# Weight halves in a three-buffer staging pool, a fourth buffer in five pools, casts and copies dealt out anew to ScalarE and VectorE, q of two more tiles by DMA transpose

## The chip, the cores and the metric

The kernel runs on one core of one Trainium2 chip. The core has four compute engines that the profile names PE (matrix multiply), DVE (vector), ACT (activation) and POOL (GpSimd), and SP, which here only issues DMAs. Each engine takes its instructions in its own fixed order and waits on semaphores for the others. The metric is the device time of one execution in microseconds. The kernel before took 172.4 us (median of 4 runs, 172.18 to 172.47).

## The reference

Attention with a sliding window of 128 positions and 4 sink positions, and after it a channel mix. There are 4 sequences of 768 positions, 8 heads of 64, so a model width of 512; the inner width of the mix is 1024.

```python
scores = q @ k.T / sqrt(64)                 # per sequence and head
keep = is_sink | (0 <= row - col < 128)
a = exp(where(keep, scores, -1e9)); a = a / a.sum()
x = (a @ v)                                 # heads side by side: [4, 768, 512]
x_prev = x shifted down by one position (0 at the start)
xk = mu_k * x + (1 - mu_k) * x_prev
xr = mu_r * x + (1 - mu_r) * x_prev
out = sigmoid(xr @ w_r) * (relu(xk @ w_k) ** 2 @ w_v)
```

All inputs and the output are float32.

## The kernel before

The positions are cut into 12 units of 256 (three a sequence, `U = 12`, u counts them). For each unit the program does this, in bf16 with sums in fp32:

- **Load and prepare** (`load`, L354; `prepare`, L516). k, q and v of the unit come in as fp32 (tiles `ks`, `qs`, `vs`), all on SP's queue. k and q are cast to bf16 by halves of four heads (`kb`, `qb`, L526 and L529: one helper, two layouts), and turned so that the head dimension lies on partitions (`kt`, `qt`). That is done in one of two ways. Either PE does four 128x128 transposes a half into a PSUM bank (L550) and another engine copies the bank out (`evacuate`, L560); or, for the units in `KD` and `QD`, a transposing DMA on SP does it (L537, `DMA_TRANSPOSE` in the profile). For such units k or q is loaded in two DMAs of 256 KB, otherwise in one of 512 KB. v is cast in two halves (`vb`, L575).
- **Attend** (`attend`, L613). Scores for two head pairs at once (L635, into `sc`), exponential on ACT (`e`, L657), times a mask on DVE (L671), value products on PE (L694, and for the sinks L682), then on DVE the reciprocal of the row sum (`rec`, L707) and the multiply (`x`, L710). A unit that is not first in its sequence also reads k and v of the unit before, and the sinks' scores (L611, `es`).
- **Mix** (`mix`, L719). PE transposes x (L733), a copy brings it to `xt` (L744), DVE takes the difference with the previous position (`td`, L758) and makes `xk` and `xr` (L768, eight instructions a unit).
- **The products** (`ffn`, L807). Key products (L818, 32 matmuls a unit in four groups of two), ReLU on ACT (`rl`, L827), square on DVE (`kk`, L831), gate products (L841, tanh on ACT L847), output products (L859) and the last multiply (`ob`, L868), which SP stores (L875).

The weights come once. `wk32`, `wr32` and `wv32` hold them whole in fp32; they are loaded in five DMAs of 1 MB (L397) and cast in ten pieces on DVE (`cast`, L492).

The order of the work is not left to a scheduler at run time. The program first records every operation in a list (class `Plan`, `op`, L135), numbered as they are recorded, with its engine, cost, the tiles that it takes from a pool, and what it reads and writes. `ORDER` (L43) is a table of these numbers for each engine, written out by hand or by a search: each engine issues its operations in just that order. `schedule` (L141) walks the five lists with the costs to decide how the lists interleave, which buffer of a pool each operation gets, and where PE would be idle for more than 0.3 to 0.6 us; there it puts a fill, a matmul on a constant tile `warm` (L879) whose result is not used. Fills are put only in the first 45 us of its reckoning. Where a pool has no free buffer, an operation waits for the one that held it.

Engines are given by small tables: `CAST` and `CAST0` (casts of k and q; the second for unit 0), `EVAC0` (copies from PSUM of unit 0; ACT for all others), `WCAST` (weights: all DVE), `VCAST` (v: DVE for unit 0, POOL for the others). `KD` is units 4 to 11, `QD` units 8 to 11.

Of the kernel before, what the change touches and what calls it, by code (L numbers as in the profile page):

```python
# [17 lines left out]
CAST = {"k": "ACT", "q": "ACT"}  # L18

CAST0 = {"k": "DVE", "q": "DVE"}  # L20
EVAC0 = {"k": "ACT", "q": "DVE", "x": "ACT"}

KD = range(4, 12)
QD = range(8, 12)
# [11 lines left out]
LOADS = ("kq0", "v0", "kq1", "wka", "v1", "wkb", "wr", "wva", "wvb")  # L36
WCAST = ("DVE",) * 10
VCAST = ("DVE", "POOL")
# [6 lines left out]
        92, 89, 98, 105, 95, 116, 108, 113, 128, 141, 124, 119, 131, 137, 103, 148, 134, 157,  # L45
        155, 168, 219, 211, 207, 212, 220, 208, 160, 176, 165, 171, 183, 189, 215, 193, 200,
        223, 180, 216, 225, 237, 298, 186, 290, 302, 291, 303, 299, 294, 248, 295, 227, 235,
        231, 263, 232, 228, 260, 306, 266, 318, 240, 256, 245, 251, 310, 276, 269, 311, 283,
        326, 329, 308, 321, 314, 343, 315, 370, 378, 352, 366, 371, 379, 332, 367, 374, 382,
        337, 375, 384, 359, 348, 386, 396, 387, 421, 390, 274, 444, 391, 452, 445, 453, 426,  # L50
        407, 448, 456, 394, 449, 457, 460, 399, 464, 404, 465, 415, 462, 410, 430, 472, 499,
        578, 437, 468, 474, 504, 469, 525, 583, 526, 537, 485, 538, 533, 509, 529, 534, 530,
        477, 553, 482, 488, 493, 545, 511, 564, 518, 549, 541, 546, 543, 550, 601, 609, 605,
        602, 556, 610, 606, 567, 631, 613, 561, 572, 614, 617, 587, 619, 621, 594, 629, 622,
        634, 625, 639, 626, 642, 677, 689, 678, 681, 663, 690, 682, 645, 707, 685, 650, 686,
        695, 701, 670, 718, 705, 702, 693, 697, 710, 698, 760, 715, 761, 756, 768, 757, 769,
        721, 726, 764, 742, 765, 772, 749, 740, 784, 780, 774, 781, 795, 834, 830, 835, 842,
        831, 787, 843, 838, 792, 798, 860, 776, 803, 816, 839, 777, 823, 846, 848, 854, 858,
        855, 871, 910, 918, 906, 911, 907, 850, 863, 851, 919, 868, 936, 874, 914, 879, 915,
        930, 892, 924, 899, 931, 926, 947, 934, 922, 944, 939, 927, 976, 972, 977, 984, 973,  # L60
        985, 950, 980, 955, 958, 981, 988, 990, 965, 992, 996, 993, 997, 1012, 1000, 1013, 1004,
        1001, 1005, 1008, 1016, 1009, 1020, 1018, 1021, 1028, 1024, 1029, 1025,
    ),
    "DVE": (
        70, 91, 88, 93, 97, 71, 94, 99, 100, 107, 112, 101, 123, 109, 114, 110, 118, 115, 120,
        125, 143, 121, 126, 146, 144, 78, 145, 150, 79, 151, 152, 81, 164, 154, 104, 159, 147,
        175, 170, 161, 80, 162, 177, 166, 178, 167, 172, 153, 173, 82, 83, 202, 195, 196, 210,
        69, 197, 203, 204, 198, 206, 84, 85, 205, 199, 214, 218, 239, 293, 301, 222, 86, 305,
        87, 255, 297, 250, 233, 244, 229, 241, 242, 257, 246, 247, 252, 258, 253, 325, 320, 278,
        312, 279, 285, 280, 287, 322, 286, 327, 323, 328, 331, 316, 281, 289, 288, 282, 354,  # L70
        333, 334, 336, 369, 373, 338, 355, 339, 377, 361, 381, 362, 356, 363, 388, 275, 357,
        392, 364, 365, 398, 358, 403, 447, 451, 414, 455, 400, 459, 401, 409, 405, 406, 466,
        416, 417, 411, 412, 432, 433, 434, 439, 441, 440, 435, 470, 442, 481, 476, 528, 436,
        510, 487, 492, 478, 532, 479, 483, 443, 489, 484, 494, 490, 495, 540, 555, 560, 513,
        536, 514, 520, 516, 515, 522, 521, 547, 551, 523, 571, 517, 566, 557, 558, 604, 524,
        568, 569, 562, 563, 573, 574, 608, 633, 612, 616, 589, 592, 590, 638, 623, 635, 591,
        596, 598, 597, 627, 636, 640, 641, 593, 599, 644, 600, 665, 649, 646, 680, 692, 647,
        684, 651, 652, 714, 666, 688, 709, 672, 667, 674, 703, 668, 675, 673, 711, 725, 699,
        712, 676, 716, 720, 669, 717, 722, 723, 727, 759, 728, 763, 744, 767, 745, 751, 771,
        746, 753, 752, 741, 786, 782, 747, 755, 791, 797, 788, 789, 833, 793, 799, 802, 794,  # L80
        800, 748, 804, 845, 805, 754, 837, 778, 841, 825, 818, 821, 819, 820, 826, 829, 827,
        867, 856, 862, 822, 878, 909, 864, 873, 865, 852, 913, 869, 870, 875, 876, 880, 828,
        881, 917, 921, 894, 943, 897, 932, 895, 938, 896, 901, 905, 902, 945, 903, 940, 941,
        928, 949, 946, 954, 904, 951, 952, 898, 956, 975, 957, 960, 979, 961, 963, 987, 962,
        983, 967, 969, 970, 968, 971, 994, 964, 998, 1003, 1007, 1015, 1011, 1022, 1030, 1026,
    ),
# [185 lines left out]
def kernel(  # L272
# [36 lines left out]
    for name in ("ks", "qs", "vs"):  # L309
        pool(name, 3, [128, 2, H, D] if name == "vs" else [128, H, 2, D], FP32)  # L310
# [620 lines left out]
```

The softmax here doesn't subtract the row's maximum and nothing guards it: scores larger than these inputs give would overflow.

## Time and profile before

| what | us |
|---|---|
| time, median of 4 runs | 172.4 |
| time of the profiled execution | 172.41 |
| its span, first to last instruction | 170.7 |
| PE busy | 161.5 |
| DVE busy | 148.4 |
| ACT busy | 132.4 |
| POOL busy | 25.5 |
| fills (L879), 42 in the record, busy | 12.4 |
| share of 16 DMA engines' span in SP's queue | 85.2% |

The profile comes from one execution, and the views used below are these. The page gives busy time by engine and 40 equal slices of the span, each digit a busy share in tenths. The groups of instructions give, by line and tile, how many there were, their busy time and the mean of one. The chain of waits follows the work back from the last instruction, each step to what released it; its columns are start, length, and who. The busy time by stage gives, for each stretch of the span, its length, the busy time of an engine with its instructions in brackets, the granted share of the PE clock (1.00 all through), the DMA engines' share and the GB/s moved. The timeline gives single instructions with their starts. A duration is from start to end; instructions of one engine overlap by some 0.1 us, so what one costs in a full queue is the distance from start to start, which is smaller (a k cast on DVE lasts 0.42 and costs 0.34; a DVE instruction on 512 fp32 from PSUM lasts 0.68 and costs 0.60).

### The profile page before, as it was taken

What the parts mean: (1) busy time and instruction counts of PE and PEld (TensorE: products, weight loads), DVE (VectorE), ACT (ScalarE), POOL (GpSimd) and SP (SyncE); (2) the same over time, 40 slices, a digit from 0 to 9 for tenths busy, and PEclk for the clock granted to TensorE, in tenths of its full rate; (3) what the DMA queues carried; (4) which work ended last, traced back from release to release, by engine and by line L of the source; (5) the groups of instructions that cost most, each with busy time, mean ns of one, the idle gap of its engine ahead of it and who ended that gap; (6) DMA issues with size and microseconds to landing.
All of it is one profiled execution on the core that took longest, in us unless ns stands there. A gap on an engine that the chain in (4) does not pass through costs nothing.

```text
span 170.7 us, 4214 instructions
## 1 busy us (share of the span) xinstructions
PE 161.5 (95%) x1603; PEld 107.9 (63%) x1624; DVE 148.4 (87%) x372; ACT 132.4 (78%) x219; POOL 25.5 (15%) x47
## 2 busy tenths in 40 slices
PE   7798988999999999999999999999999999999992
PEld 2345566575758567767658668577585775684751
DVE  2497989999999778899999999998999989999632
ACT  3169987999999999999879979978887938654330
POOL 6130070006200020124201100110300113000000
PEclk9999999999999999999999999999999999999999
DMA  4999999999949899999767998998997975030203
GB/s 96 242 272 377 289 293 356 353 285 214 296 108 216 225 255 252 158 229 209 189 145 140 257 234 183 219 126 208 167 223 193 188 204 150 0 127 0 108 15 123
DMA packets 82803, 33.82 MB, mean 198 GB/s; under 512 B 64736, under 2 KB 77280, under 8 KB 82784
## 3 DMA queue, kind: packets, MB, share of 16 engines
q1 hardware_dynamic: 81728, 33.56, 85.2%
q8 instruction: 12, 0.20, 0.6%
q10 hardware_dynamic: 1056, 0.00, 0.3%
q14 instruction: 7, 0.06, 0.1%
HBM read 24.12 MB, written 6.29 MB: 178 GB/s over the span
## 4 chain that ended last, share of the span: by engine, by line
PE 81%; DMA 6%; SPq 6%; POOL 1%; issue 1%; ACT 1%; DVE 1%
PE bank L818 24%; PE bank L859 23%; PE bank L841 11%; DMA vs<-in_v_dram 6%; PE sc L635 6%; PE bank L694 6%; PE bank L733 3%; SPq L377 3%; PE bank L550 2%; SPq L360 2%; PE bank L682 2%; PE bank L611 2%; POOL vb L575 1%; SPq L397 1%; PE bank L788 1%
## 5 line engine op out<-in xcount | busy, mean ns | idle before, releaser
L657 ACT ACTIVATE e<-sc 128x1024 bf16<-128x1024 f32 (+1 forms) x48 | 45.0, 975 | 5.2 <-PE sc L635 5.2
L818 PE MATMUL bank<-xk,wk_sb 128*128 128x256 bf16 x384 | 48.9, 273 | 0.0
L859 PE MATMUL bank<-wv_h,kk 128*128 128x512 bf16 x173 | 45.4, 379 | 0.6
L818 PEld LDWEIGHTS <-wk_sb 128*128 128x128 bf16 x384 | 35.7, 98 | 7.1 <-issue 0.2
L575 POOL CAST vb<-vs 128x512 bf16<-128x512 f32 x22 | 18.8, 861 | 110.8 <-DMA vs<-in_v_dram 82.3
L827 ACT ACTIVATE rl<-bank 128x512 bf16<-128x512 f32 x48 | 27.6, 608 | 9.1 <-PE bank L818 8.4
L671 DVE TENSOR_TENSOR e<-e,mask 128x1024 bf16<-128x1024 bf16 (+1 forms) x48 | 30.5, 645 | 0.8 <-ACT e L657 0.8
L859 PEld LDWEIGHTS <-kk 128*128 128x128 bf16 x184 | 16.7, 98 | 14.7 <-DVE kk L831 0.3
L831 DVE TENSOR_TENSOR kk<-rl 128x512 bf16<-128x512 bf16 x48 | 21.4, 458 | 4.5 <-ACT rl L827 4.3
L841 PE MATMUL bank<-wr_sb,xr 128*128 128x512 bf16 x88 | 23.9, 379 | 0.8 <-DVE wr_sb L503 0.4
L768 DVE SCALAR_TENSOR_TENSOR xk<-td,mu,xt 128x256 bf16<-128x256 bf16 x48 | 22.7, 499 | 0.2
L768 DVE SCALAR_TENSOR_TENSOR xr<-td,mu,xt 128x256 bf16<-128x256 bf16 x48 | 22.5, 484 | 0.1
L710 DVE TENSOR_TENSOR x<-bank,rec 128x256 bf16<-128x256 f32 x48 | 19.6, 418 | 0.6
L694 PE MATMUL bank<-vb,e 128*128 128x65 bf16 x352 | 18.9, 193 | 0.9 <-POOL vb L575 0.9
L694 PEld LDWEIGHTS <-e 128*128 128x128 bf16 x352 | 16.8, 97 | 3.2 <-issue 1.0
L847 ACT ACTIVATE th<-bank 128x512 f32<-128x512 f32 x24 | 14.1, 602 | 5.0 <-PE bank L841 4.8
L868 DVE SCALAR_TENSOR_TENSOR ob<-th,bank 128x512 f32<-128x512 f32 x23 | 15.7, 682 | 2.2 <-ACT th L847 1.7
L744 ACT COPY xt<-bank 128x512 bf16<-128x512 bf16 x24 | 14.1, 593 | 4.2 <-PE bank L733 3.8
L841 PEld LDWEIGHTS <-xr 128*128 128x128 bf16 x96 | 9.0, 98 | 8.2 <-issue 0.4
L635 PE MATMUL sc<-qt,kt 64*128 64x128 bf16 (+1 forms) x256 | 14.0, 238 | 0.0
L879 PE MATMUL bank<-warm 128*128 128x512 bf16 x42 | 12.4, 426 | 1.4 <-DVE warm L894 1.3
L635 PEld LDWEIGHTS <-kt 64*128 64x128 bf16 x256 | 8.9, 94 | 6.0 <-issue 3.7
(54 smaller groups left out, 158.4 us busy)
## 6 DMA issues: line engine op xcount, KB each, us to landing
vs<-in_v_dram SPq DMA_DIRECT2D x24, 256.0 KB, 4.9
out_dram<-ob SPq DMA_DIRECT2D x23, 256.0 KB, 3.4
ks<-in_k_dram SPq DMA_DIRECT2D x18, 256.0 KB, 4.9
qs<-in_q_dram SPq DMA_DIRECT2D x7, 512.0 KB, 6.0
qs<-in_q_dram SPq DMA_DIRECT2D x10, 256.0 KB, 4.3
wk<-in_moe_w_k_dram SPq DMA_DIRECT2D x2, 1024.0 KB, 8.6
wv<-in_moe_w_v_dram SPq DMA_DIRECT2D x2, 1024.0 KB, 11.3
ks<-in_k_dram SPq DMA_DIRECT2D x3, 512.0 KB, 7.4
```

The source lines that it names most:

```text
L575: lambda g=g, copy=copy: copy(out=buf["vb", u][:, g, :, 0:D], in_=buf["v", u][:, g, :, :]), rank,
L635: nc.tensor.matmul(out=sc[:, a, o0:o1], lhsT=lhs[rows], rhs=rhs[rows], start=True, stop=True)
L657: nc.scalar.activation(out=buf[ek][:, :, lo:], in_=buf[sck][:, :, lo:], func=AF.Exp, scale=scale)
L671: nc.vector.tensor_tensor(out=at, in0=at, in1=m, op=ALU.mult)
L694: nc.tensor.matmul(out=o[:, g, a, :], lhsT=e[:, a, e0:e0 + 128], rhs=rhs, start=(T == 0 and i == 0), stop=(i == len(blocks) - 1), skip_gro ...
L710: P.op("DVE", dve(256), lambda ok=ok, rk=rk, c=c: nc.vector.tensor_tensor(out=buf["x", u][:, :, 128 * c:128 * c + 128].rearrange("p g (a d ...
L768: nc.vector.scalar_tensor_tensor(out=buf[key][:, c0 + i, :], in0=buf[tk][:, i, :], scalar=mu[w][:, c0 + i:c0 + i + 1], in1=xt[:, c0 + i, t ...
L818: nc.tensor.matmul(out=ps[:, i, :], lhsT=wk_sb[:, c, 128 * f:128 * f + 128], rhs=xk[:, c, :], start=(c == 0), stop=(c == NC - 1), skip_gro ...
L827: P.op("ACT", act(512), lambda psk=psk, rk=rk: nc.scalar.activation(out=buf[rk], in_=buf[psk].rearrange("p (i t) -> p i t", i=2), func=AF. ...
L831: P.op("DVE", dve(512, 0.52), lambda f2=f2, rk=rk: nc.vector.tensor_tensor(out=buf["kk", u][:, 2 * f2:2 * f2 + 2, :], in0=buf[rk], in1=buf ...
L841: nc.tensor.matmul(out=buf[psk], lhsT=buf["xr", u][:, c, 128 * g:128 * g + 128], rhs=wr_sb[:, c, :], start=(c == 0), stop=(c == NC - 1))
L859: nc.tensor.matmul(out=buf[psk], rhs=wv_h[:, f, :], lhsT=buf["kk", u][:, f, 128 * g:128 * g + 128], start=(f == 0), stop=(f == NF - 1))
```

## The change

- **Staging.** `wk32`, `wr32` and `wv32` go. A pool `w32` of three 1 MB buffers takes the five weight loads in turn; a load waits until the casts of the one before it in its buffer are done.
- **Pools.** `qt`, `xk`, `vb`: four buffers instead of three; `kk`: three instead of two; `rl`: five instead of four. A unit's `kk` buffer is now taken with the first ReLU instead of the first square.
- **Engines.** Casts, copies and ReLUs get alternatives (`alts`), and a table `CHOICE` from operation number to engine picks among them. By instruction: k casts on DVE 2 before, 10 after; q casts on DVE 2 and 8; copies of `kt` on DVE 0 and 4, of `qt` 2 and 3, of `xt` 0 and 2; ReLUs on DVE 0 and 4 (as a maximum with 0); v casts on POOL 22 and 12, on ACT 0 and 8, on DVE 2 and 4; weight casts on DVE 10 and 6, on ACT 0 and 4. Together ACT's operations fall by 17 and DVE's rise by 24.
- **q by DMA transpose** for units 6 to 11 instead of 8 to 11: 16 transposes on PE and 4 copies on ACT go, 4 transposing DMAs come, and two q loads of 512 KB become four of 256 KB.
- **Order.** `ORDER` is new for all five engines, and with it the number of fills falls from 44 to 34. On SP the start is now: k and q of unit 0 by halves in turn, v of unit 0, k and q of unit 1, first half of v of unit 1, q of unit 2, both halves of w_k, second half of v of unit 1, k of unit 2, w_r, v of unit 2, w_v. Before, w_k's halves stood ahead of both halves of v of unit 1, and q of unit 2 behind them. On DVE the constants' memsets now come ahead of the first q cast. The two small loads of `mu` stand on ACT's queue behind the first and the third cast or copy of unit 1 instead of at its head. Scores of units 4 and 5 stand earlier among PE's work than before.
- **Reckoned costs** in the plan (issue time of a DMA on SP, its service time, a POOL cast) are changed; they have a bearing only on interleaving, buffers and fills.

```diff
-CAST = {"k": "ACT", "q": "ACT"}
-CAST0 = {"k": "DVE", "q": "DVE"}
-EVAC0 = {"k": "ACT", "q": "DVE", "x": "ACT"}
+CHOICE = {
+    82: "ACT", 85: "ACT", 87: "ACT", 89: "ACT", 90: "DVE", 92: "DVE", 93: "DVE", 95: "DVE", 98:
...
 KD = range(4, 12)
-QD = range(8, 12)
+QD = range(6, 12)
...
-LOADS = ("kq0", "v0", "kq1", "wka", "v1", "wkb", "wr", "wva", "wvb")
-WCAST = ("DVE",) * 10
-VCAST = ("DVE", "POOL")
+LOADS = ("kq0", "v0", "kq1", "wka", "wkb", "v1", "wr", "wva", "wvb")
...
 ORDER = {
...
     "SP": (
-        1, 3, 0, 2, 4, 5, 6, 7, 8, 11, 9, 10, 16, 12, 15, 13, 20, 14, 19, 17, 18, 21, 22, 25,
...
+        1, 0, 3, 2, 4, 5, 6, 7, 10, 16, 8, 9, 11, 15, 12, 17, 18, 13, 14, 19, 20, 25, 23, 21,
...
+        i = len(self.ops)
+        if i in CHOICE:
+            engine = CHOICE[i]
+            cost, emit, port = alts[engine]
...
+    pool("w32", 3, [128, NC, 512], FP32)
-    pool("qt", 3, [128, NP, 2, 128], BF16)
+    pool("qt", 4, [128, NP, 2, 128], BF16)
-    pool("xk", 3, [128, NC, 256], BF16)
+    pool("xk", 4, [128, NC, 256], BF16)
-    pool("kk", 2, [128, NF, 256], BF16)
-    pool("rl", 4, [128, 2, 256], BF16)
+    pool("kk", 3, [128, NF, 256], BF16)
+    pool("rl", 5, [128, 2, 256], BF16)
-    pool("vb", 3, [128, 2, H, D + 1], BF16)
+    pool("vb", 4, [128, 2, H, D + 1], BF16)
...
-    wk32 = tile1([128, NC, Dff], FP32, "wk32")
-    wr32 = tile1([128, NC, Dm], FP32, "wr32")
-    wv32 = tile1([128, NF, Dm], FP32, "wv32")
...
+        key = ("w32", name, i)
+        P.op("SP", 1000.0, lambda: nc.sync.dma_start(out=buf[key], in_=src), rank,
+             service=2880.0, descs=512, take=[("w32", key)], writes=[(name + "32", i)])
...
+    def cast(out, name, i, cut, rank, writes):
+        key = ("w32", name, i)
+        half = name == "wv"
+        def emit(by):
+            if by == "ACT":
+                return lambda: nc.scalar.activation(out=out, in_=buf[key][cut], func=AF.Copy,
+                                                    scale=0.5 if half else 1.0)
+            if half:
+                return lambda: nc.vector.tensor_scalar(out=out, in0=buf[key][cut], scalar1=0.5,
+                                                       scalar2=None, op0=ALU.mult)
+            return lambda: nc.vector.tensor_copy(out=out, in_=buf[key][cut])
...
+            def relu_dve(psk=psk, rk=rk):
+                nc.vector.tensor_scalar_max(
+                    out=buf[rk], in0=buf[psk].rearrange("p (i t) -> p i t", i=2), scalar1=0.0)
+
+            P.op("ACT", act(512), relu, rank + f2,
+                 alts={"ACT": (act(512), relu, False), "DVE": (dve(512), relu_dve, False)},
+                 take=[("rl", rk)] + ([] if f2 else [("kk", ("kk", u))]),
```

## The prediction

> **What bounds the kernel now.** I read the page first: busy shares and the 40 slices.
>
> ```profile
> PE 161.5 (95%) x1603; PEld 107.9 (63%) x1624; DVE 148.4 (87%) x372; ACT 132.4 (78%) x219; POOL 25.5 (15%) x47
> PE   7798988999999999999999999999999999999992
> DVE  2497989999999778899999999998999989999632
> ACT  3169987999999999999879979978887938654330
> DMA  4999999999949899999767998998997975030203
> ```
>
> TensorE (PE) is full from the seventh slice on; DVE is nearly full from the same place; DMA is full in the first third. Where PE is idle, the busy time by stage tells:
>
> ```profile
> 0.00:24.00 24.00, 20.83 (x172) 1.00 1.01 255
> 24.00:28.00 4.00, 2.84 (x54) 1.00 1.06 345
> 28.00:32.00 4.00, 3.30 (x27) 1.00 1.08 356
> 32.00:44.00 12.00, 11.95 (x120) 1.00 1.06 277
> 44.00:160.00 116.00, 115.14 (x1190) 1.00 0.85 177
> ```
>
> From 32 to 160 us PE misses 0.9 us in 128. So the end is "when the start-up lets PE go" plus the PE work behind that point. Much of the busy time before 24 us is fill (42 matmuls on `warm`, 12.4 us busy), which computes nothing. What lets PE go is in the chain of waits:
>
> ```profile
> 11.99 11.03 DMA vs<-in_v_dram
> 23.07 2.53 POOL vb L575
> 25.64 0.28 PE bank L694 x4
> ...
> 165.74 1.76 PE bank L788 x16
> 167.52 0.42 DVE ob L798
> ```
>
> The second half of v of unit 1 lands at 23.02, POOL casts it until 25.60, the value products of unit 1 start at 25.64 and end at 26.99; the last matmul ends at 167.5, then 3.2 us of last multiply and store. DVE has this cover left behind the start-up (busy time by stage):
>
> ```profile
> 28.00:44.00 16.00, 15.57 (x33) 1.00 1.06 297
> 44.00:60.00 16.00, 14.83 (x43) 1.00 0.91 204
> 60.00:80.00 20.00, 17.72 (x39) 1.00 1.28 223
> 80.00:100.00 20.00, 19.76 (x53) 1.00 0.89 188
> 100.00:120.00 20.00, 18.82 (x50) 1.00 0.90 189
> 120.00:140.00 20.00, 19.14 (x48) 1.00 0.92 189
> 140.00:160.00 20.00, 18.96 (x48) 1.00 0.24 73
> ```
>
> 124.8 busy of 132: 7.2 us idle. Its best 20 us were 98.8% busy.
>
> **The change, part by part.** The sum is made against the profiled execution: span 170.7, own time 172.41 (1.7 around the span), the median of the runs shown is 172.40.
>
> *Less PE work.* q of units 6 and 7 goes through the DMA crossbar: 4 groups of 4 transposes leave PE, 0.22 us a group in the chain: **-0.88**. They lie where PE is never idle, so all of it is on the path. With them go 4 evacuations of ACT (0.58 start to start). Two q loads of 512 KB become four of 256 KB, and 4 transposing DMAs come to SP's queue (1.2 us of issue each, 3.2 to landing): 4.9 us plus two issues of 0.53. SP waited 10.1 and 6.0 us on ACT ahead of its transposes, so it has that time. Upper bound: scores of unit 5 stand about 8 us earlier in PE's order than before, and their k transposes landed only 2.0 us ahead of use (71.8 against 73.84), so the loads must move up as much; the queue order does that (k of unit 5 is transposed at places 37 and 39 of SP instead of 44 and 45). I take 0, up to +1.5.
>
> *The start-up gate.* SP's order becomes: k, q of unit 1, first half of v of unit 1, q of unit 2, both halves of w_k, second half of v of unit 1. In the trace these same transfers all landed by 24.59 (q of unit 2: issued at 15.69, 8.9 to landing), one behind another. So the last of them, now v, lands near 24.6 instead of 23.0. Its cast moves from POOL (2.53 us here, 0.62 where nothing is in the way) to DVE (0.42 before): ready at 25.05, value products from 25.15, end near 26.65: **-0.34**. What is done by then is equal: ahead of it PE now has two q groups and the sink scores of unit 2 (0.22 + 0.22 + 0.44), and misses one pair of key products (0.87). So ten fewer fills give nothing by themselves: the gate is a DMA. The faster beginning (first k cast after its load at about 5.7 instead of 6.9, the 1.9 us of memsets moved into DVE's first wait, evacuations on both engines: scores of unit 1 near 16 instead of 18.2) ends in the same gate and counts 0. Bounds: v landing as early as before (-1.5 in all), or everything one transfer later (1.6 us for q of unit 2: +1.3).
>
> *The staging pool.* w_v's halves wait for the casts of w_k's (three buffers). Reckoned as above, w_k's first half lands near 19.3 and is cast by 22.8; SP's queue is by then still some 8 us of transfers ahead of the landings, so no hole opens. w_r and the first half of w_v land some 1.6 us later than before, and the gate and output products that read them now stand behind seven key products of unit 1 (PE reaches them near 34 and 38, w_v lands near 34.0 and 36.8). Hence 0, and the 0.4 that PE waited for w_r can go. With the 0.5 on a k cast and on x, the idle time between 27 and 32 is 0.8; I take none of it, since DVE takes it again (next).
>
> *The spread.* Behind the gate DVE gets 9 k casts and 5 q casts (0.34 start to start), 2 v casts (0.34), one x evacuation (0.6, as a q evacuation on DVE in the trace), 4 ReLUs; it loses 3 weight casts (0.60). A ReLU on DVE is not in the trace: between 0.34 (`kk`, 512 columns from SBUF) and 0.72 (q evacuation from PSUM); 0.60 as `ob`, which also reads 512 fp32 from PSUM. Sum: 3.06 + 1.7 + 0.68 + 0.6 + 2.4 - 1.8 = +6.6 us. Against it, POOL makes 12 v casts instead of 22. Beside POOL the squares took up to 0.83 instead of 0.42; over `kk`, `xk` and `e` I count some 0.2 us lost a POOL cast, 8 fewer behind the gate: -1.6. Net +5.0 on 7.2 idle. DVE then needs 129.8 of 132: **98.3%**, where 98.8% is the best that it did. ACT is relieved by some 8 us, but had little to do with the end: PE waited on it for 0.3 us after 24. So DVE is late next, against PE's key products (`xk`) and output products (`kk`). At 98.8% it costs 0; at 95.7% (the 120 to 140 row) 129.8/0.957 = 135.6, +3.6. I take **+0.5**, nearer the pressed rows.
>
> On POOL and DVE the Trainium skill ("SBUF — State Buffer", Who interferes with whom) says that a GpSimd read and a DVE cast or two-input instruction exclude each other for a whole instruction. By that rule each cast removed from POOL could give back up to a whole cast, 0.6 us instead of my 0.2, and the spread would cost some 3 us less DVE time; the sum goes by the trace's 0.2.
>
> *Deeper pools* (`qt`, `xk`, `kk`, `rl`, `vb`, one buffer each): PE showed no wait over 0.15 us after 44 us, so there is nothing to take away: 0.
>
> *mu* moves behind a k cast on ACT's queue (issue near 12.6 instead of 0.8). It landed 3.6 and 4.6 us after issue: 17.2, where DVE wants it near 17.5. From that instruction to the last mask ahead of the gate DVE has 6.5 us of work, and the gate is at 24.65: 0 as long as mu lands by 18.1.
>
> *Fewer fills at the very start* (8 instead of 12). The matmul pitch on fills was 0.43 at first. The first transposes come sooner after the shorter row, so PE is hardly idle longer: 0. The rule against it is in "TensorE: Matmul & The Clock Gate", Part 1 of the skill: about 3.4 us of sustained work before the clock is full. By it, should the shorter row miss the window, some 1.1 us of transposes and scores would run at half speed, +1.1, inside a lead that the gate swallows: again 0.
>
> Sum: -0.88 - 0.34 + 0.5 = -0.7: span 170.0, time **171.7**.
>
> **The rivals.**
> *All covers hold* and the 0.8 of idle time at 27 to 32 goes as well, DVE costing nothing: -0.88 - 0.34 - 0.8 = -2.0: 170.4. For it: DVE does 98.8% when pressed. Against: before, it was pressed so for 20 us, now for 130.
> *DVE becomes the bound* (the other side). At 97% its 129.8 us take 133.8, +1.8, less the 0.34 that it starts earlier: 173.9. It decides from 98.1% down, where 129.8/s passes 132.34. For it: in-order waits on PE and ACT cost DVE 7.2 us here, and its order is packed throughout. Against: much of that idle time was slack that PE's pace left, and a further 2.5 us of idle time lies at 160 to 164, behind the last `xk`.
> *DVE eats the whole gain*: 172.4.
> *A late load at the start*: mu behind loaded queues. SP's loads took 8.9 to 11 us to land there; with 10.9 mu lands at 23.5, 5.4 after the limit: up to +4.7, and half of that likelier: 174. Against: the 8.9 is time behind its own queue, and ACT's queue is empty.
>
> **How the numbers follow.** Forecast (170.9 to 172.0) 0.46; all covers hold 0.16; gain eaten 0.11; DVE bound 0.19; late load 0.08. A change of under 0.2% (0.34 us) can't be told from none. Faster: 0.42 of the first and all of the second, 0.58; same: the third and an edge of the first, 0.13; slower 0.29. The range leaves out the early v landing (below 170.2) and DVE under 97%, or mu more than 2 us late (above 174.0).
>
> **What would show it.** Right: value products of unit 1 released by DVE's `vb` near 25; PE idle under 1.5 us from 27 to 160; DVE over 97% from 28 to 150; 48 q transposes on PE; fewer fills, but idle in their place. Wrong: PE waiting on `xk` or `kk` of DVE in many places (DVE bound); DVE standing before the first `xk` for mu; PE waiting for `qt` or `kt` by DMA at units 5 to 8; or PE's gate well before 25, which would say that the order of loads is worth more than the sum of transfers tells.

## The result, and the profile after

The changed kernel took 172.8 us (median of 53 runs, 170.5 to 174.8) against 172.45 for the kernel before (74 runs, 171.7 to 173.4). The ratio of the two is 0.9998, its 95% interval 0.9988 to 1.0008; it takes only runs up to 1.5% above the fastest of their kernel, which leaves out the 14 longest of the changed kernel and none of the kernel before, and over all runs the medians differ by +0.2%. So there is no gain, and perhaps a small loss, where 171.7 us and a ratio of 0.996 were forecast.

Yet the profiled execution did nearly what was forecast up to its last matmul. Where nothing else is said, the lines below are of it: time 172.48, span 170.17. The page first: busy shares and slices.

```profile
PE 159.5 (94%) x1579; PEld 105.6 (62%) x1598; DVE 155.3 (91%) x396; ACT 126.2 (74%) x202; POOL 16.0 (9%) x37
PE   7887779999999999999999999999999999999992
DVE  7899979999999999999999999999799899999831
```

DVE is busy for 6.9 us more and POOL for 9.5 us less; DVE is now nearly full from the start. The busy time of PE by stage:

```profile
0.00:24.00 24.00, 18.83 (x161) 1.00 0.99 260
24.00:28.00 4.00, 3.57 (x60) 1.00 0.94 311
28.00:32.00 4.00, 3.71 (x45) 1.00 1.04 278
32.00:44.00 12.00, 11.88 (x110) 1.00 1.15 305
44.00:160.00 116.00, 114.82 (x1170) 1.00 0.84 184
```

Two microseconds of fills are gone from the first row without harm, and from 24 to 32 PE is busier (7.28 of 8 instead of 6.14). The chain of waits, around the gate and at the end:

```profile
13.10 10.53 DMA w<-in_moe_w_k_dram
23.63 0.02 issue
23.65 0.69 DVE wk_sb L509
24.34 0.60 DVE e L687
24.95 0.34 DVE vb L587
25.29 0.60 DVE e L687
...
165.46 1.32 PE bank L806 x12
166.79 0.02 issue
166.81 0.42 DVE ob L816
```

The gate is still a transfer, but now the second half of w_k (landed 23.63), followed by DVE instructions in a row: the cast of w_k, a mask, and the cast of v (landed 24.73). With the end of that cast, at 25.29, the value products start. The chain itself goes on along DVE until 31.27, where PE waited 0.29 us for `xk`. DVE by stage, from 28 us:

```profile
28.00:44.00 16.00, 15.86 (x39) 1.00 1.12 298
44.00:60.00 16.00, 15.82 (x44) 1.00 0.90 198
60.00:80.00 20.00, 19.11 (x48) 1.00 1.04 218
80.00:100.00 20.00, 19.82 (x54) 1.00 1.06 199
100.00:120.00 20.00, 19.36 (x52) 1.00 0.85 191
120.00:140.00 20.00, 18.15 (x47) 1.00 0.86 202
140.00:160.00 20.00, 19.23 (x50) 1.00 0.33 97
```

127.35 of 132 us busy (124.81 before), and up to 99% in a stage, with PE idle for only 0.6 us behind 27 us (1.0 before; pieces over 0.12 us).

How the two executions stand against each other:

| us | before | after | difference |
|---|---|---|---|
| end of the value products of unit 1 | 26.99 | 26.87 | -0.12 |
| from there to the last matmul's end | 140.49 | 139.90 | -0.59 |
| last matmul's end to the end of the span | 3.22 | 3.40 | +0.18 |
| time outside the span | 1.71 | 2.31 | +0.60 |

The value products run in groups of four. Before, one group was done ahead of the gate, and seven were left (the first and the last group; the second starts at 25.64):

```profile
24.43 0.28 PE L694 MATMUL bank<-vb,e 128*128 128x65 bf16 x4
26.71 0.28 PE L694 MATMUL bank<-vb,e 128*128 128x65 bf16 x4
```

After, all eight stand behind the gate, 0.18 us apart, and this is the last:

```profile
26.59 0.28 PE L710 MATMUL bank<-vb,e 128*128 128x65 bf16 x4
```

So 0.71 was won by the last matmul, just the forecast's 0.7, and given back behind it, most of it outside the span, where the profile has no instruction. (0.18 behind the last matmul is not explained.) Over all runs of the changed kernel the time outside the span is 2.3 (2.01 to 2.48), where the kernel before has 1.7 (1.66 to 2.03 in 125 runs), so this is no accident of one execution. The spans differ less than in the profiles: their medians are 170.7 and 170.5, and those of the changed kernel spread from 168.1 to 172.3. There are two questions, then: what adds 0.6 outside the span, and what takes most of the 0.7 inside it in most executions, where the median span is only 0.2 shorter.

### The profile page after: what moved, and what is told of

Its sections match the earlier page's. It is cut to its first block, busy times and chain, and to the rows that moved or that the text cites. A ratio compares the mean times of both kernels' runs of the same rounds, so it can differ in the third digit from the quotient of the medians.

```text
span 170.2 us, 4167 instructions
## 1 busy us (share of the span) xinstructions
PE 159.5 (94%) x1579; PEld 105.6 (62%) x1598; DVE 155.3 (91%) x396; ACT 126.2 (74%) x202; POOL 16.0 (9%) x37
## 4 chain that ended last, share of the span: by engine, by line
PE 59%; DMA 14%; SPq 11%; DVE 10%; ACT 2%; issue 2%; POOLq 0%; DVEq 0%; ACTq 0%
PE bank L836 18%; PE bank L885 16%; PE bank L867 9%; DMA w<-in_moe_w_k_dram 6%; PE bank L710 4%; PE sc L651 4%; SPq L387 4%; DMA vs<-in_v_dram 3%; DMA qs<-in_q_dram 3%; SPq L370 3%; DMA out_dram<-ob 2%; PE bank L749 2%; SPq L380 2%; DVE e L687 2%; PE bank L698 1%
## 5 line engine op out<-in xcount | busy, mean ns | idle before, releaser
L836 PE MATMUL bank<-xk,wk_sb 128*128 128x256 bf16 x384 | 50.1, 273 | 1.9 <-DVE wk_sb L509 1.5
L673 ACT ACTIVATE e<-sc 128x1024 bf16<-128x1024 f32 (+1 forms) x48 | 44.4, 959 | 1.9 <-PE sc L651 1.7
L846 ACT ACTIVATE rl<-bank 128x512 bf16<-128x512 f32 x44 | 25.7, 601 | 12.7 <-PE bank L836 12.4
L786 DVE SCALAR_TENSOR_TENSOR xr<-td,mu,xt 128x256 bf16<-128x256 bf16 x48 | 23.1, 494 | 0.0
L858 DVE TENSOR_TENSOR kk<-rl 128x512 bf16<-128x512 bf16 x48 | 19.5, 418 | 0.9 <-ACT rl L846 0.8
L710 PE MATMUL bank<-vb,e 128*128 128x65 bf16 x352 | 19.7, 193 | 0.4 <-DVE e L687 0.3
L758 ACT COPY xt<-bank 128x512 bf16<-128x512 bf16 x22 | 12.9, 589 | 6.6 <-PE bank L749 6.4
L587 POOL CAST vb<-vs 128x512 bf16<-128x512 f32 x12 | 8.6, 718 | 85.1 <-DMA vs<-in_v_dram 80.8
L698 PE MATMUL bank<-vsink,es 128*128 128x130 bf16 x64 | 12.5, 220 | 0.2 <-DVE x L726 0.2
```

The source lines that it names most:

```text
L673: nc.scalar.activation(out=buf[ek][:, :, lo:], in_=buf[sck][:, :, lo:], func=AF.Exp, scale=scale)
L710: nc.tensor.matmul(out=o[:, g, a, :], lhsT=e[:, a, e0:e0 + 128], rhs=rhs, start=(T == 0 and i == 0), stop=(i == len(blocks) - 1), skip_gro ...
L786: nc.vector.scalar_tensor_tensor(out=buf[key][:, c0 + i, :], in0=buf[tk][:, i, :], scalar=mu[w][:, c0 + i:c0 + i + 1], in1=xt[:, c0 + i, t ...
L836: nc.tensor.matmul(out=ps[:, i, :], lhsT=wk_sb[:, c, 128 * f:128 * f + 128], rhs=xk[:, c, :], start=(c == 0), stop=(c == NC - 1), skip_gro ...
L846: nc.scalar.activation(out=buf[rk], in_=buf[psk].rearrange("p (i t) -> p i t", i=2), func=AF.Relu)
L858: P.op("DVE", dve(512, 0.52), lambda f2=f2, rk=rk: nc.vector.tensor_tensor(out=buf["kk", u][:, 2 * f2:2 * f2 + 2, :], in0=buf[rk], in1=buf ...
```

## The experiments

First each kernel again, unchanged.

> The kernel before, unchanged, for its span beside its time. In the profiled execution on record 1.7 us lay outside the span (172.41 against 170.7), in the changed kernel's 2.3 (172.48 against 170.2). Theory A (the 0.6 belongs to the changed program: in its trace two 8 KB instruction fetches run at 171.8 and 172.4, behind the last instruction at 170.2, and the kernel before has none there): 1.7 again, no fetch behind the last instruction. Theory B (it varies from execution to execution): anything from 1.7 to 2.4.

172.64 us, ratio 1.0023 (1.0003 to 1.0044), outside the span 1.71.

> The changed kernel, unchanged. Theory A: span 169.5 to 170.6, 2.2 to 2.4 us outside it, ratio to before 0.998 to 1.002. Theory B: the time outside the span is as in the kernel before.

173.16 us, ratio 1.0044 (1.0017 to 1.007), outside the span 2.36, profiled span 171.07. Two kernels that are the same can thus differ by 0.2%; what follows rests on terms that are read apart (outside the span, single waits), and on times only where they are larger.

**Outside the span.** The trace holds the DMAs that fetch instructions: 16 KB at a time on queue q8, which keep step with PE's instructions, and 8 KB on q14, which the runs below tie to DVE and POOL. Inside the span the page counts 7 on q14 before:

```profile
q14 instruction: 7, 0.06, 0.1%
```

and 6 after:

```profile
q14 instruction: 6, 0.05, 0.1%
```

The changed kernel's other two start at 171.79 and 172.38, one behind the other, 1.6 and 2.2 us behind its last instruction (170.17); before, the last started at 138.0. For each fetch one can count how many instructions each engine had issued by then. POOL's total fell from 79 to 64, DVE's rose from 415 to 445, ACT's fell from 294 to 280. The first two experiments give ACT and POOL back what they had lost, by instructions that nothing uses.

```diff
         nc.vector.memset(warm, 0.0)
+        for _ in range(14):
+            nc.scalar.copy(out=pad[:, 0:16], in_=warm[:, 0:16])
```

> The changed kernel with 14 tiny copies (16 columns) ahead of ACT's first work, where ACT waits for its first load until 6.7 us; they bring ACT's instruction count back to that of the kernel before and touch nothing else. Theory A, if it is ACT's code that is fetched at the end: the fetches behind the last instruction go or move into the run, the time outside the span falls to 1.7, time near 171.9 (ratio 0.997). If it is another engine's: no change, 2.3 outside. Theory B: no change either.

173.41 us, 2.30 outside, both fetches still behind the end (174.07 and 174.42): not ACT.

```diff
         nc.vector.memset(warm, 0.0)
+        for _ in range(15):
+            nc.gpsimd.memset(pad[:, 0:16], 0.0)
```

> The same on POOL: 15 tiny memsets (16 columns) ahead of POOL's first work, which bring its instruction count back to that of the kernel before. POOL's first result that PE needs is ready at 2.1 and needed at 5.5 us, so the span should stay at 170.2 within 0.4. Theory A, if it is POOL's code that is fetched at the end: 1.7 outside the span, time near 171.9 (ratio 0.997). Otherwise no change.

173.27 us, 2.08 outside (2.02 to 2.14), one fetch behind the end; the other had come in at 116, with POOL at 69. One of the two is POOL's. The next run pads DVE as well.

```diff
+        for _ in range(15):
+            nc.gpsimd.memset(pad[:, 0:16], 0.0)
+        for _ in range(16):
+            nc.vector.memset(vpad[:, 0:16], 0.0)
```

> The changed kernel with 15 tiny memsets on POOL and 16 on DVE ahead of their first work. They compute nothing that is used. Theory A (the second of the two instruction fetches behind the end belongs to DVE's queue, the first to POOL's, as the run with POOL's pad alone showed): both fetches move into the run, none behind the end, time outside the span 1.7 instead of 2.3; the memsets (about 0.06 us each, 1 us in all) lie in DVE's wait for the first load or move the start by up to 0.5, which the gate at 25 swallows; time 172.3 to 172.6. Rival B (the second belongs to SP or to no engine's count): one fetch is left behind the end, outside the span 2.1, time 173.0.

No fetch behind the end, 1.71 outside (1.66 to 1.75), as before the change. The second was DVE's: with 16 more it comes when DVE has issued 446, and without them DVE has 445 in all. The time, 172.74 us, hardly fell, since these pads lie at the start; so the next run puts them late, where both engines are idle.

```diff
+    P.op("POOL", 400.0, lambda: [nc.gpsimd.memset(ppad, 0.0) for _ in range(8)], 900.0)
+    P.op("DVE", 400.0, lambda: [nc.vector.memset(vpad, 0.0) for _ in range(6)], 900.0)
...
...
 POOL:
-    735, 737, 736,
+    735, 737, 736, 1030,
...
 DVE:
-    1013, 1009, 1020,
+    1013, 1009, 1031, 1020,
```

> The changed kernel with 8 tiny memsets on POOL behind its last cast and 6 on DVE behind its last square, where DVE stood 1.9 us (162.8 to 164.7). They compute nothing that is used. With POOL's and DVE's counts of 64 and 445 the two fetches ran behind the end; in the run with pads at the start they ran when POOL had issued 69 and DVE 446. Theory A (the end waits for the fetches): both come inside the run, time outside the span 1.7 instead of 2.3, the span as without pads (median 170.5): time 172.2, ratio 0.9985, 0.6 below the changed kernel. Rival B (the 0.6 goes back into the span, since the run with pads at the start had a median span of 171.0): time 172.7.

173.21 us, ratio 1.0029 (1.0003 to 1.0055): slower, although 1.70 outside. DVE's fetch now ran at 168.47 to 168.98, beside the last store, and from the last matmul to the end of the span it took 4.36 us instead of 3.40. A fetch in that place costs more than one behind the end. With more pads it comes earlier:

```diff
-    P.op("POOL", 400.0, lambda: [nc.gpsimd.memset(ppad, 0.0) for _ in range(8)], 900.0)
-    P.op("DVE", 400.0, lambda: [nc.vector.memset(vpad, 0.0) for _ in range(6)], 900.0)
+    P.op("POOL", 400.0, lambda: [nc.gpsimd.memset(ppad, 0.0) for _ in range(16)], 900.0)
+    P.op("DVE", 400.0, lambda: [nc.vector.memset(vpad, 0.0) for _ in range(14)], 900.0)
```

> The changed kernel with 16 tiny memsets on POOL behind its last cast and 14 on DVE in its wait of 1.9 us near 163 (6 took 0.74 there). DVE's fetch should then come near 164 instead of 168.5, ahead of the last store, and POOL's near 124. Theory A (the end waits for fetches behind it, and a fetch beside the last store lengthens that store): outside the span 1.7, from the last matmul to the end of the span 3.4 instead of 4.4, span 170.5, time 172.2, ratio 0.9985. Rival B (pads move the time elsewhere): span 171 or more, time as the changed kernel, 172.8.

172.27 us, ratio 0.9991 (0.9965 to 1.0017). The page's row of the queue, and on the timeline DVE's pads in its idle time ahead of the last multiplies (start, length, instruction):

```profile
q14 instruction: 8, 0.07, 0.2%
```

```profile
163.15 1.81 DVE L927 MEMSET vpad<- 128x8 uint32 x14
165.14 0.69 DVE L899 SCALAR_TENSOR_TENSOR ob<-th,bank 128x512 f32<-128x512 f32 x1 [0.18 <-issue]
```

All eight fetches are inside (POOL's at 124.6, DVE's at 161.0), the tail is back at 3.4, 1.69 are left outside and the span is 170.6: 0.5 us below the changed kernel, as theory A had it. The times outside the span, together:

| kernel | start of fetches behind the last instruction, us behind it | outside, median |
|---|---|---|
| before | none | 1.71 |
| changed | 1.6 and 2.2 | 2.3 |
| POOL padded | 1.6 | 2.08 |
| casts back on ACT (below; DVE 22 instructions fewer) | 1.9 | 1.89 |
| q of unit 2 late, two kernels (below; DVE 1 instruction fewer) | 1.8 and 1.8 to 1.9 | 1.96; 1.96 |
| single loads earlier (below; DVE 1 instruction fewer) | 1.7 and 1.8 | 2.00 |
| POOL and DVE padded late | 0.3 | 1.70 |
| POOL and DVE padded at the start; padded in DVE's wait | none | 1.71; 1.69 |

Without a fetch behind the end it is 1.7. With two it is 2.3 where the second starts 0.35 to 0.6 us behind the first, but 2.0 where they start within 0.13 us of each other, so the number of fetches alone does not set it.

**Inside the span.** The executions differ in the stretch from 100 to 120 us. The waits of DVE and PE there in the repeated run of the changed kernel (total, times, longest):

```profile
DVE ob L894 <- DMA out_dram<-ob: 1.0, 1, 1.0
```

```profile
PE bank L698 <- DVE ob L894: 0.6, 1, 0.6
```

DVE's last multiply stands for a store that still reads the `ob` buffer it wants, and PE for the bank that this multiply frees; in the run with ACT padded, 1.3 and 0.9, and PE waited 0.7 more for k of unit 9. In the profile after, the first is 0.3 and PE does not wait. The cause stands on SP's queue 8 us earlier. In the profile after:

```profile
100.44 1.19 SPq L552 DMA_TRANSPOSE kt<-kb  x1
101.67 1.25 SPq L380 DMA_DIRECT2D ks<-in_k_dram  x1
102.97 0.57 SPq L370 DMA_DIRECT2D vs<-in_v_dram  x1
103.59 1.17 SPq L901 DMA_DIRECT2D out_dram<-ob  x2
```

and in the repeated run:

```profile
100.81 2.49 SPq L552 DMA_TRANSPOSE kt<-kb  x1
103.36 0.57 SPq L380 DMA_DIRECT2D ks<-in_k_dram  x1
103.99 0.57 SPq L370 DMA_DIRECT2D vs<-in_v_dram  x1
104.60 1.31 SPq L901 DMA_DIRECT2D out_dram<-ob  x2
```

One transpose (second half of k of unit 8) took 2.5 us to issue instead of 1.2, and all behind it on SP, the store among them, was late. The next kernel takes away what DVE waits for, by a fourth buffer.

```diff
-    pool("ob", 3, [128, Dm], FP32)
+    pool("ob", 4, [128, Dm], FP32)
```

> The changed kernel with four buffers for `ob` instead of three, nothing else. In three of four executions of the changed kernel DVE stood 1.0 to 1.3 us at 108 us for the store of an `ob` buffer, and PE then 0.6 to 0.9 us for a bank that `ob` frees; PE waited another 0.7 to 0.9 us near 118 for the DMA transposes of k of unit 9. Theory A (SP's queue is late there, its stores hold DVE and its transposes hold PE): the wait on the store is gone in this run, PE idle behind 27 us falls to 1.2 us or less from 0.5 to 2.1, and the median span falls by some 0.4 us to 170.2; time outside the span stays 2.3; time 172.3, ratio 0.999. Rival B (the transposes alone set the pace there, the store's wait lies inside that delay): the wait at 108 goes but reappears before the scores of unit 9, span 170.7, time 173.0, ratio 1.003. Rival C (the spans spread because of the start-up): nothing changes, 172.9.

172.64 us, ratio 1.001 (0.9985 to 1.0035), median span 170.3. The transpose was long again (2.65), the wait on the store is gone, PE's waits at 108 and 118 too. But the next late load shows, on ACT, behind which exponentials stand:

```profile
ACT vb L587 <- DMA vs<-in_v_dram: 2.4, 1, 2.4
```

PE was idle for 1.8 us behind 27 us all the same. So neither theory A nor B: the store's wait was real and worth little alone, since SP's queue is late for all that hangs on it. Moving single loads forward as well, still with four `ob` buffers, does no better:

```diff
 SP:
+    k/9/0
     kt/8/0  qt/8/1  kt/8/1
-    k/9/0
...
+    v/10/0
     st:ob/6/1  qt/10/0  qt/10/1  kt/10/0  kt/10/1
-    v/10/0
```

> The changed kernel with four `ob` buffers, and on SP's queue the load of the first half of k of unit 9 ahead of the first DMA transpose of k of unit 8 (two transposes and a long third earlier), and the load of the first half of v of unit 10 five places earlier. Theory A (loads that stand behind transposes and stores on SP hold ACT and DVE, and they PE, in most executions): none of the waits on a store (DVE, 1.0 to 1.3 us), on k and q of unit 9 (PE) and on v of unit 10 (ACT, 2.4 us with four `ob` buffers alone) is left; PE idle behind 27 us below 1.0 us; span 170.0 or less, time 172.2, ratio 0.9985. Rival B (what goes here comes back at the next unit, because SP as a whole is too slow): span 170.5 or more, another wait on DMA of over 0.5 us at units 9 to 11.

172.62 us, ratio 0.9993 (0.9968 to 1.0019). PE waited 0.7 for the transposes of k and 0.7 for a bank: rival B, the waits move on. Together with the late pads:

> The two before put together: four `ob` buffers, the two loads earlier on SP's queue, the pads on POOL and DVE at the end. If both causes are told rightly they add: span 170.0, outside it 1.7, time 171.7, ratio 0.996, which is the time that was forecast for the change. Rival (the waits are moved only): 172.2, ratio 0.9985.

173.68 us, ratio 1.0056 (1.0031 to 1.0081): the fetch beside the last store again, as in the run of the late pads.

Why is that transpose long? In eight profiles of the changed kernel and of variants with the same work on PE it was 2.4 to 2.65 us where a fetch of PE's instructions began 0.73 to 0.80 us behind the start of its issue (six of them), 1.19 where it began at 0.80 (the profile after, where the next issue took 1.25 instead of 0.57), and 1.19 where it began at 1.39 (late pads). There too the next issue, a load, was long, 1.47 instead of 0.57, and DVE stood 0.6 us for the store:

```profile
101.99 1.47 SPq L385 DMA_DIRECT2D ks<-in_k_dram  x1
```

All 20 profiles together, with 544 transposing DMAs (many of them the same ones in kernels that differ little), say the same. Where a 16 KB fetch began between 0.5 us ahead of the start of the issue and 0.83 behind it, 55 of 59 issues took over 1.5 us; where it began 0.83 to 1.05 behind it, 1 of 16. With no such fetch from 1.5 us ahead to 2 us behind, 62 of 411 took over 1.5 us, so there is another cause besides. The fetches come every 256 instructions or so of PE, so they can be moved by instructions alone:

```diff
+    def fill(bank):
+        fills.append(bank)
+        if len(fills) > 8:
+            nc.tensor.matmul(out=bank, lhsT=warm[:, 0:128], rhs=warm, start=True, stop=True)
+            return
+        for i in range(7):
+            nc.tensor.matmul(out=bank[:, 64 * i:64 * i + 64], lhsT=warm[:, 0:128],
+                             rhs=warm[:, 0:64], start=True, stop=True)
```

> The changed kernel with each of the first 8 fills split in seven matmuls of 64 columns: the same PE time, 96 instructions more, so that each of PE's instruction fetches comes some 5 us earlier (the one at 101.2 to 101.8 near 96.5). Theory A (a transpose's issue on SP takes 2.4 us instead of 1.2 when a 16 KB fetch of PE begins from its start to 0.77 us behind it): the second transpose of k of unit 8 is issued in 1.2, DVE does not wait for the store at 108, PE does not wait at 108 nor at 118; span 170.2 or less, unless a fetch falls on another transpose; time 172.4. Rival B (the long issue comes from the traffic of other transfers or the wait for the cast): still 2.4 us, span 170.5 to 171.

172.03 us, ratio 0.9986 (0.9956 to 1.0016); median span 169.6 (169.1 to 171.4), outside it still 2.34. The fetch came at 95.8, and on SP's timeline:

```profile
100.49 1.21 SPq L552 DMA_TRANSPOSE kt<-kb  x1
101.75 0.57 SPq L380 DMA_DIRECT2D ks<-in_k_dram  x1
102.37 0.57 SPq L370 DMA_DIRECT2D vs<-in_v_dram  x1
102.99 1.38 SPq L901 DMA_DIRECT2D out_dram<-ob  x2
```

No wait for the store, PE's wait at 108 down to 0.2, none at 118. All of PE's fetches moved, so how much of the 0.9 us belongs to this one is not told apart. Both causes taken away at once:

```diff
+    P.fill = fill
+    P.op("POOL", 400.0, lambda: [nc.gpsimd.memset(ppad, 0.0) for _ in range(16)], 900.0)
+    P.op("DVE", 400.0, lambda: [nc.vector.memset(vpad, 0.0) for _ in range(14)], 900.0)
```

> The changed kernel with the first 8 fills split (as a_peshift) and the pads on POOL and DVE (as a_pad3). If the two causes are all that stood between the forecast and the measurement, they add: span 169.6 to 169.9, outside it 1.7, time 171.3 to 171.6, ratio 0.994 to 0.9955. Rival (a_peshift's span was luck of one call): span 170.5, time 172.2, ratio 0.9985.

171.59 us (171.08 to 172.42), ratio 0.9959 (0.9934 to 0.9984): faster than the kernel before by 0.4% (8 runs), and than the changed kernel's 172.8; span 169.8, outside 1.74. PE, by stage:

```profile
24.00:28.00 4.00, 3.96 (x65) 1.00 1.04 325
28.00:32.00 4.00, 4.00 (x46) 1.00 1.02 279
32.00:44.00 12.00, 11.85 (x115) 1.00 1.09 296
44.00:160.00 116.00, 114.77 (x1167) 1.00 0.88 184
```

The same split of the fills in the kernel before:

> The kernel before with its first 8 fills split in the same way, nothing else: every fetch of PE comes some 5 us earlier. Theory A (SP's lead is what the change used up: in the kernel before, where three transposes met a fetch, a late SP held neither DVE nor PE): the same span, 170.7, time 172.4, ratio 1.000. Rival B (the fetches cost the kernel before as much): span 170, time 171.7, ratio 0.996.

172.49 us, ratio 1.0017 (0.9993 to 1.004), span 170.8: nothing is gained. The kernel before had long transposes too (3.34 at 77.4, 2.2 at 65.0), but DVE never stood for a store there.

**Parts of the change undone.** q of units 6 and 7 by PE again:

```diff
-QD = range(6, 12)
+QD = range(8, 12)
```

(and in the order the four pieces on PE, their copies on ACT and two loads on SP, at the times where their counterparts ran).

> The changed kernel with q of units 6 and 7 turned by PE again (16 transposes, 4 copies on ACT, two loads of 512 KB instead of four of 256 KB, four DMA transposes fewer on SP's queue). The forecast's term: 0.88 us more work on PE where it is never idle: span +0.9, time 173.7, ratio 1.007. Rival B (SP's queue pays for the four transposes: with them gone the stores and the transposes of unit 8 and 9 come in time): DVE's wait on the store at 108 and PE's waits at 108 and 118 go, -0.6 to -1.6: time 172.0 to 173.0, ratio 0.998 to 1.003. Rival C (the copies on ACT, 0.6 us each, make PE wait): ratio above 1.010.

175.51 us, ratio 1.0217 (1.0161 to 1.0274): rival C. The waits of PE behind 28 us:

```profile
PE bank L835 <- ACT rl L845: 0.9, 1, 0.9
PE bank L866 <- ACT qt L572: 0.8, 1, 0.8
```

Against the profile after, the stretch behind the gate is 3.3 us longer; 1.9 of that is idle time (2.5 instead of 0.6) and 1.4 the transposes themselves with the short gaps around them. PE's fetches move in this run too.

14 casts of k and q and three ReLUs back from DVE to ACT, each at its place in time:

```diff
-    261: "DVE", 267: "DVE",
+    261: "ACT", 267: "ACT",
...
-    886: "DVE",
+    886: "ACT",
```

> The changed kernel with 14 of the casts of k and q behind the gate and three ReLUs moved from DVE back to ACT, at the places in time where DVE did them. DVE loses 14 x 0.34 + 3 x 0.6 = 6.6 us of work of some 127, ACT gains about 10 us. The forecast's term (DVE pressed costs PE 0.5 us): span -0.5, time 172.4, ratio 0.999. Rival B (DVE's 96.5% was slack that PE's pace leaves, cost nothing): the same time, 172.9, ratio 1.002, DVE's busy share behind 28 us falls to 91.5% and nothing else moves. Rival C (ACT's in-order queue then delays the transposes on SP, which wait for its casts): PE waits on `kt` or `qt` by DMA, 173.4 or more, ratio above 1.005.

177.0 us, ratio 1.0233 (1.0181 to 1.0285). PE was idle for 2.5 us behind 27 (pieces over 0.12 us), but DVE was busy for only 117.1 of 132 us (127.35 in the profile after): it stood for ACT, 3.5 us for exponentials and 2.4 for ReLUs, and of PE's waits behind 28 us 2.0 were for ACT and 0.5 for DVE. The casts cost more on ACT than on DVE, by far, in this order of work. How much of the 4 us is theirs alone is not told apart: the plan also set five fills behind the gate in this kernel (36.1 to 41.6 us), 1.5 us of PE's queue, where the changed kernel has none.

**The gate.** q of unit 2 behind the second half of v of unit 1:

```diff
 SP:
     v/1/0
-    q/2/0
     wk32/0  wk32/1  v/1/1
+    q/2/0
```

(and its casts, transposes, copies and the sinks' scores of unit 2 behind the value products of unit 1).

> The changed kernel with q of unit 2 loaded behind the second half of v of unit 1 instead of ahead of w_k; its two casts on DVE, its transposes and the sinks' scores on PE and the copies on ACT stand behind the value products of unit 1. The forecast's step on the gate: it is the sum of the transfers, so v lands 1.6 us earlier (23.1), the value products start at 23.6 instead of 25.3, and 0.88 us of PE work moves behind them: span -0.8, time 172.0, ratio 0.998. Rival B (the gate is DVE's work: it was busy 4.00 of 4 us from 24 to 28, and the squares, masks and casts ahead of the value products set the time): v lands at 23.1 but the products start at 24.5 or later, 0.88 us of work is added: span 0 to +0.9, time 172.8 to 173.7, ratio 1.002 to 1.007.

177.25 us, ratio 1.0284 (1.025 to 1.0318). v landed at 22.56 instead of 24.73, but:

```profile
DVE xk L791 <- DMA mu<-in_moe_mu_k_dram: 4.3, 1, 4.3
```

mu's first load, issued at 11.2, took 9.5 us to land and DVE stood for it, which is the forecast's fourth rival, in another kernel. With mu loaded first on ACT, as before the change:

> As the run with q of unit 2 loaded behind the second half of v of unit 1, and with the two loads of mu first on ACT's queue, as the kernel before has them. In the run without that, v landed at 22.6 instead of 24.7, but mu at 20.7 instead of 16.6, and DVE stood 4.3 us for it. The forecast's step on the gate (the sum of the transfers): DVE does not wait for mu, value products of unit 1 start near 23.4 instead of 25.3, 0.88 us of PE work moves behind them: span 169.5, time 171.8, ratio 0.9965. Rival B (DVE's work ahead of the products sets the gate): they start at 24.5 or later, span 170.5 or more, ratio 1.000 to 1.007.

175.16 us, ratio 1.0172 (1.0132 to 1.0212). v landed at 22.82 and the value products ended at 25.55 instead of 26.87, 1.3 us earlier. They started at 24.0, between the 23.4 of the forecast's step and the 24.5 of rival B. The work that had been moved behind them then waited for what prepares it:

```profile
PE bank L632 <- ACT qt L578: 1.1, 1, 1.1
PE bank L841 <- DVE x L731: 0.7, 1, 0.7
PE bank L841 <- DVE wk_sb L514: 0.7, 2, 0.3
```

> As a_gate2, with four `ob` buffers and the pads of a_pad3. If all three causes are told rightly: span 169.3, outside it 1.7, time 171.0, ratio 0.992. If the gate does not move: 171.9 to 172.2, ratio 0.997 to 0.999. If waits are only moved: 172.4 or more.

174.29 us, ratio 1.0128 (1.0083 to 1.0173), outside the span 1.70: the pads do their part, the gate's order costs more than it brings.

## Why the prediction was wrong, point by point

- **The step that failed first: "1.7 around the span", carried over unchanged.** It became 2.3, because POOL's and DVE's instruction counts, changed by the spread, put one fetch of each behind the last instruction. That is 0.6 us, nearly as large as the whole forecast gain; the kernels without a fetch behind the end or beside the last store give 1.7 again (1.69 to 1.74). Nothing in the profile of before showed such a fetch behind the end, but its trace has the fetches and the counts, and the change of the counts stood in the table of engines.
- **The second: SP's queue, "I take 0, up to +1.5".** The four transposes were costed by SP's idle time and by one landing (k of unit 5), not by the slack of what else is queued: stores that free `ob` buffers, which stayed at three, and loads. Where one issue lasted 1.25 us longer, DVE stood 0.9 to 1.3 us for a store in four of five profiles with three `ob` buffers, and PE up to 1.6 in all; the profiled execution of the changed kernel happened to miss it. With all of PE's fetches moved the median span is 0.7 to 0.9 lower (169.6 and 169.8 against 170.5); what part of that is this one issue is not told apart. With both causes gone the time is 171.59, and the forecast was 171.7.
- **The agreement up to the last matmul is partly luck.** The sum had -0.34 at the gate and -0.38 behind it (-0.88 and +0.5); the profile shows -0.12 and -0.59.
- **Less PE work, -0.88.** Right in sign, and not too large: undone, it cost 2.7 us of time against the changed kernel, and of the stretch behind the gate 1.4 was PE's own.
- **The gate, -0.34.** It came out at -0.12. v landed at 24.73 (forecast 24.6) and its cast ended at 25.29 (25.15 for the start), and the eight groups of value products ended at 26.87 (26.65). The forecast was right that the second half of v, cast on DVE, lets the value products go, and right in kind that the landing follows the sum of the transfers: v came at 22.56 and 22.82 with q of unit 2 behind it, even earlier than the 23.1 expected.
- **The spread, +0.5.** The waits of PE over 0.12 us behind 27 us fell from 1.0 to 0.6 (the prediction counted 0.8 before, where its own parts give 0.9). With -0.88 of work that would make some -1.25 where -0.59 was measured, so 0.7 went into pieces too short to be named: 0.3 in all, against the +0.5. Whether DVE took it stays open. DVE was busy for 127.35 us (126.8 in the repeated run), not 129.8, and from 28 to 150 us for 96.4%, not over 97%. A ReLU took 0.60 start to start, as assumed; the copy of `xt` 0.31 in the same measure, not 0.6. POOL had not 8 but 10 casts fewer behind the gate (20 and 10), and the squares, `td`, `xk` and `xr` together took some 3.4 us less for equal counts, 0.34 a cast instead of 0.2. By the whole-instruction exclusion of the Trainium skill ("SBUF — State Buffer", Who interferes with whom) it could have been up to 0.6 a cast; the measured 0.34 lies between, and the runs do not separate what else changed. "ACT was relieved but had little to do with the end" was wrong for the new order: with the casts back on ACT the time is 4 us longer, in a kernel that also has five fills more.
- **mu, 0 "as long as it lands by 18.1".** It landed at 16.6, 0.2 ahead of the first `xk`; the run with another order of loads shows what the rival would have cost, 4.3 us of DVE.
- **Staging pool, deeper pools, fewer fills: 0.** No wait of PE behind the gate names them; PE's clock was granted in full in all stages.
- **The rivals.** Neither "DVE becomes the bound" nor "DVE eats the gain" happened, though the second gave nearly the right time, 172.4, for a wrong reason.

## What to carry to other kernels

A change that moves instructions between engines also moves the points where each engine fetches its next block of instructions: look in the trace for fetches behind the last instruction, beside the last store and beside the issue of a transposing DMA, and count the time outside the span as a term of its own. When DMAs are added to an in-order queue, price the lateness of everything behind them, stores that free buffers too, and not the queue's idle time. A median over many executions can miss a gain that one profile shows, when a wait of a microsecond hangs on a few hundredths of one.

## What was not expected of the hardware

- An 8 KB fetch that starts 1.6 to 1.9 us behind the last instruction keeps the execution open: 1.89 and 2.08 us outside the span with one, 2.3 with two in turn, 1.96 to 2.00 with two that start together, 1.7 with none or with one that starts at 0.3.
- DVE's fetches come 128 issued instructions apart or nearly so (190, 317 and 446 in the run padded at the start), PE's about 250 (matmuls and weight loads together, the mean of the profile after).
- A fetch (0.5 us) beside the last store lengthened the tail from 3.40 to 4.36 us.
- The issue of a transposing DMA mostly lasted over 1.5 us instead of 1.2 where a 16 KB fetch began from 0.5 us ahead of its start to 0.83 behind it (55 of 59 in 20 profiles; 1 of 16 where it began 0.83 to 1.05 behind). For one of them the cause is shown by moving the fetch away: 2.4 to 2.65 us with it, 1.2 in both runs without. The mechanism is open, and some issues are long with no fetch near (62 of 411).
